# First loads and last transposes of an attention stage, put in another order

## The chip, the cores and the metric

The kernel runs on one core of one Trainium2 chip. The metric is the device time of one execution in microseconds (us); lower is better. A core has a matrix engine (TensorE, PE in the profile, with its weight loads as PEld), a vector engine (DVE), an activation engine (ACT), GpSimd (POOL) and a sync engine (SP), which here issues every transfer between DRAM and on-chip memory on one queue. Each engine runs its own instructions strictly in the order in which the program gives them, and waits where an operand is not there yet.

## The reference, cut to what matters

Attention inside chunks of 64 positions, then a soft mixture of experts on its result, then a gated feed-forward layer. All is float32; the last layer's weights are float64.

```python
def _attn_ref(q, k, v):                   # B, H, S, D = 8, 8, 576, 64
    scores = scale * np.matmul(q_c, k_c.transpose(0, 1, 2, 4, 3))   # chunks of 64
    scores = scores - np.max(scores, axis=-1, keepdims=True)
    attn = np.exp(scores)
    attn = attn / (np.sum(attn, axis=-1, keepdims=True) + 1e-09)
    out = np.matmul(attn, v_c)

def _moe_ref(x, phi, w1, w2):             # x is 4608 x 512, 8 experts of 4 slots
    logits = x @ phi
    d = np.exp(logits - logits.max(0, keepdims=True))
    d /= d.sum(0, keepdims=True) + 1e-09
    slot_input = d.T @ x
    # each expert e: slot_out[e] = np.maximum(slot_input[e] @ w1[e], 0) @ w2[e]
    # c = softmax of logits over the slots
    return c @ slot_out

def _moe2_ref(x, w_gate, w_val, w_out):   # 512 -> 1536 -> 512
    g = x @ w_gate
    return (g / (1.0 + np.exp(-g)) * (x @ w_val)) @ w_out
```

## The kernel before, in words

The order of every engine's instructions is the order in which the kernel is written (the scheduler is off). There are three stages.

**Stage one** is the attention with the token softmax of the mixture over all positions, run online. There are 36 tiles of 128 rows, taken in 18 passes (`p`) of two. Of tile `i` the queries and keys lie together in one of three buffers `qkbd` (`qk_bd[i % 3]`; part 0 holds the queries, parts 1 and 2 the keys of the upper and lower 64 partitions, each with zeros in the other half), its values in one of three buffers `vbd`. `load_qk` brings queries and keys into parts 0 and 1; `spread_k` then copies the lower half of part 1 into part 2 and clears what it copied from, and `spread_v` does the same with the values. Both run on POOL, but for the spread of tile 0's keys, which is DVE's.

A tile goes through `emit_scores` (8 products on PE into `s_ps`, then maximum and subtraction on DVE into `ssb`), `emit_pt` (4 transposes, exponential on ACT), `emit_pv` (products with the values into `xa_ps` and `xb_ps`; DVE scales them into `x_sb`, one for the two tiles of a pass), `emit_xt` (4 transposes into `xt_ps`; ACT copies them into `xt`). Four tiles make a group `g`, of which there are 9: `emit_logits` (16 products with `phi` into `lt_ps`, then running maximum and exponential), `emit_et` (one transpose, `e_ps`) and `emit_si` (4 products into `si_ps`, which DVE adds to `acc` with a factor). `load_qk(i + 3)` stands behind `emit_scores(i)` and waits for it, since it writes into the same buffer; `load_v(i + 3)` stands behind the products of tile `i` in the same way. So the sync engine's queue moves at the pace of PE, and PE waits for what the queue brings.

At the end of each pass `pump(1)` issues one load for the later stages: first `w_val`'s share (`load_gv0`; `w_gate`'s share is issued among the very first loads), then, from the third pass on, 1 MB of expert weights at a time (`w1t`, `w2t`), into 16 slots and, once stage one has released its buffers, 4 more.

The end of stage one is written out by hand: the last pass takes the first half of the last group's logits (tiles 32 and 33), adds up group 7, then transposes tiles 34 and 35, takes the second half of the logits, and goes through `emit_m1` (`mps`, the maximum over the four rows of a slot), `emit_et(8)`, `emit_m2` (`nps`, and the factor `al`, and from it `rsel`) and `emit_si(8)`. `warm(n)` puts in `n` products of the identity with itself, whose result nobody reads. The tag `t` has three PSUM buffers, which all the small results named here share.

**Stage two** is the experts: `sips` (L607) turns `acc` into the slots' inputs, then the products with `w1t` (`h_ps`, L636) and `w2t` (`so_ps`, L681). A weight slot is loaded anew when PE has read it. **Stage three** (from about 195 us on) is the gated layer, with float64 weights split into float32 pieces on the way; nothing in it is touched by the change.

Of the kernel before, what the change touches and what calls it, by code (L numbers as in the profile page):

```python
# [34 lines left out]
def tile_attn_softmoe_swiglu(  # L35
# [239 lines left out]
    with tc.manual_schedule():  # L275
# [22 lines left out]
        for u in range(3):  # L298
            load_qk(u)
            load_v(u)  # L300
            if u == 0:
                load_gv0(0, wp)
        nc.sync.dma_start(out=phi_sb, in_=phi.rearrange("(k p) s -> p k s", p=128))

        for i in range(NK):
            nc.vector.memset(qk_bd[i][top, 2], 0.0)
            nc.vector.memset(v_bd[i][top, 1], 0.0)
            if i == 0:
                make_identity(nc, ident)
# [161 lines left out]
        def emit_si(g):  # L471
            e = e_t.pop(g)
            ps = ps_t.tile([128, 512], F32, tag="t", name="si_ps")
            for jt in range(4):
                nc.tensor.matmul(
                    out=ps[32 * jt:32 * jt + 32, :],
                    lhsT=e[:, 32 * jt:32 * jt + 32],
                    rhs=x_t.pop(4 * g + jt),
                    start=True, stop=True,
                    tile_position=(0, 32 * jt),  # L480
                )
            if g:
# [24 lines left out]
        def emit_m2():  # L507
# [8 lines left out]
            nc.scalar.activation(out=al, in_=mrun[0], func=ACTF.Exp, bias=nm)  # L516
            rsel = sm.tile([128, 32], F32, tag="rsel", name="rsel", bufs=1)
            nc.vector.tensor_scalar(out=rsel, in0=sel_big[:, 0, :], scalar1=al, scalar2=None, op0=ALU.mult)
            tail['al'] = al
# [7 lines left out]
        spread_k(0, nc.vector)  # L527
        spread_k(1)
        spread_k(2)
        spread_v(0)  # L530
        spread_v(1)
        for i in range(2):
            emit_scores(i)
            load_qk(i + NK)
        spread_k(3)
        for i in range(2):
            emit_pt(i)
        NP = NTILE // 2
        for p in range(NP):
            if p < NP - 1:  # L540
                for i in (2 * p + 2, 2 * p + 3):
                    emit_scores(i)
                    if i + NK < NTILE:
                        load_qk(i + NK)
# [13 lines left out]
            if p >= 2 and p % 2 == 0:  # L558
                emit_logits(p // 2 - 1)
            if p >= 3 and p % 2:  # L560
                if p == NP - 1:
                    emit_logits(NG - 1, (0, 1), False)
# [10 lines left out]
        emit_xt(NTILE - 2)  # L573
        emit_xt(NTILE - 1)
        emit_logits(g, (2, 3))
        warm(4)
        emit_m1()
        nc.vector.tensor_copy(out=lt_all[:, g, :], in_=lt_t[g][:, 0:128])
        emit_et(g)
        warm(3)  # L580
        emit_m2()
        emit_si(g)
# [413 lines left out]
```

## Time and profile before

| what | us |
|---|---|
| median of 3 runs | 571.0 |
| lowest and highest | 570.22 and 571.45 |
| the profiled execution, its own time | 570.47 |
| its span, first to last instruction | 568.5 |
| PE busy | 540.1 (95% of the span) |
| PEld busy | 425.8 (75%) |
| DVE busy | 419.2 (74%) |
| POOL busy | 292.1 (51%) |
| ACT busy | 260.6 (46%) |
| share of the chain that ended last: PE, DMA, DVE | 80%, 12%, 4% |

The chain that ended last is followed back from the last instruction: at each step to what released it, or to the instruction before it on its engine. Busy shares are means over stages with different limits, and a PE that stands at a wait inside a row of products still counts as busy in part; what a change in one stage is worth is read from that stage's own rows. Times inside the trace count from the span's start. The granted clock of PE stands as a share of its upper level (2.4 GHz); half of it is the lower level (1.2 GHz).

### The profile page before, as it was taken

The page shows a single profiled execution, that of the slowest core. Times are in us where ns is not written, and L with a number is a line of the kernel's source. Part 1 is how long each engine was busy: PE and PEld are TensorE (multiplying, and loading weights), DVE is VectorE, ACT ScalarE, POOL GpSimd, SP SyncE. Part 2 cuts the span into 40 slices and gives each one's busy share as a digit, 9 for nine tenths or more (in the row PEclk, how much of TensorE's full clock was granted, in tenths as well). Part 3 has the DMA queues.
Part 4 walks back from the last instruction along what each step waited for, and adds up shares of the span by engine and source line. Part 5 has one row for each costly group of instructions (what it writes and reads, how often), then busy time and mean ns, then how long its engine had stood idle before and what let it go on. Part 6 is the DMA issues. An engine that isn't in the chain of part 4 may idle for free.

```text
span 568.5 us, 10116 instructions
## 1 busy us (share of the span) xinstructions
PE 540.1 (95%) x3823; PEld 425.8 (75%) x3823; DVE 419.2 (74%) x745; ACT 260.6 (46%) x500; POOL 292.1 (51%) x322
## 2 busy tenths in 40 slices
PE   3998999999999888999999999999999999999997
PEld 2877788777543556888888878887888788888885
DVE  5678887776475599989889878997998854433464
ACT  1233333334244576666665555554555543333331
POOL 3566766663100257656756556664676454343432
PEclk9999999999999998999999999999999999999999
DMA  7799999998899970202020240024000000122254
GB/s 256 261 305 345 359 376 369 359 375 310 323 381 379 390 269 1 74 1 74 0 75 0 76 149 1 0 75 148 1 1 1 0 2 0 44 105 75 74 186 184
DMA packets 37967, 91.03 MB, mean 160 GB/s; under 512 B 3104, under 2 KB 5152, under 8 KB 37920
## 3 DMA queue, kind: packets, MB, share of 16 engines
q1 hardware_dynamic: 37920, 90.40, 44.0%
q8 instruction: 30, 0.49, 0.3%
q14 instruction: 17, 0.14, 0.1%
HBM read 80.95 MB, written 9.44 MB: 159 GB/s over the span
## 4 chain that ended last, share of the span: by engine, by line
PE 80%; DMA 12%; DVE 4%; POOL 2%; issue 1%; ACT 1%; SPq 0%; POOLq 0%; DVEq 0%; ACTq 0%
PE o L877 17%; PE o L879 17%; PE o L878 17%; DMA qkbd<-in_qk_dram 5%; PE v_ps L833 4%; DMA vbd<-in_v_dram 4%; PE g_ps L833 4%; PE s_ps L337 4%; PE xa_ps L373 3%; PE h_ps L636 3%; DMA w2t<-in_moe_w_dram 2%; PE gg_ps L814 2%; PE pt_ps L359 2%; PE xt_ps L410 2%; PE so_ps L681 1%; PE lt_ps L428 1%
## 5 line engine op out<-in xcount | busy, mean ns | idle before, releaser
L846 POOL TENSOR_TENSOR lo_sb<-s_sb,hi_sb 128x512 fp32r<-128x512 f32 x106 | 140.6, 1326 | 134.1 <-ACT hi_sb L845 131.2
L877 PE MATMUL o<-whl,hi_sb 128*128 128x512 f32 x428 | 167.9, 392 | 2.5 <-DVE part L886 2.5
L879 PE MATMUL o<-whl,lo_sb 128*128 128x512 f32 x428 | 167.3, 391 | 0.5 <-POOL lo_sb L846 0.5
L878 PE MATMUL o<-whl,hi_sb 128*128 128x512 f32 x428 | 167.1, 391 | 0.0
L836 ACT ACTIVATE s_sb<-g_ps 128x512 f32<-128x512 f32 (+1 forms) x110 | 64.8, 591 | 153.6 <-PE g_ps L833 150.4
L837 DVE TENSOR_TENSOR s_sb<-s_sb,v_ps 128x512 f32<-128x512 f32 (+1 forms) x110 | 73.9, 673 | 78.1 <-ACT s_sb L836 76.6
L877 PEld LDWEIGHTS o<-whl,hi_sb 128*128 128x128 f32 x428 | 80.8, 189 | 22.4 <-DVE part L886 4.4
L879 PEld LDWEIGHTS o<-whl,lo_sb 128*128 128x128 f32 x428 | 80.6, 188 | 17.9 <-POOL lo_sb L846 0.9
L878 PEld LDWEIGHTS o<-whl,hi_sb 128*128 128x128 f32 x428 | 80.7, 189 | 16.3
L845 ACT ACTIVATE hi_sb<-s_sb 128x512 fp32r<-128x512 f32 (+1 forms) x110 | 67.6, 616 | 0.8 <-DVE s_sb L837 0.8
L890 DVE TENSOR_TENSOR part<-part,o 128x512 f32<-128x512 f32 x92 | 57.0, 676 | 2.6 <-PE o L879 2.6
L220 POOL TENSOR_TENSOR mt<-mt,ex 128x512 f32<-128x512 f32 x32 | 39.6, 1237 | 30.5 <-PE g_ps L833 14.4
L337 PE MATMUL s_ps<-qkbd 128*64 128x128 f32 x576 | 40.5, 293 | 12.3 <-POOL qkbd L322 6.5
L337 PEld LDWEIGHTS s_ps<-qkbd 128*64 128x64 f32 x576 | 33.9, 146 | 22.3 <-POOL qkbd L322 8.3
L207 DVE SCALAR_TENSOR_TENSOR ex<-raw,ex 128x512 uint16<-128x512 uint16 x32 | 47.7, 1490 | 0.1
L833 PE MATMUL v_ps<-c_t,g_st 128*128 128x512 f32 (+1 forms) x110 | 42.9, 393 | 3.1 <-ACT s_sb L836 2.5
L833 PE MATMUL g_ps<-c_t,g_st 128*128 128x512 f32 (+1 forms) x110 | 42.4, 388 | 0.1
L412 ACT ACTIVATE xt<-xt_ps 128x512 f32<-128x512 f32 (+1 forms) x36 | 19.4, 589 | 47.7 <-PE xt_ps L410 47.6
L321 POOL COPY qkbd<-qkbd 64x512 f32<-64x512 f32 x35 | 21.4, 612 | 30.5 <-DMA qkbd<-in_qk_dram 27.4
L202 DVE SCALAR_TENSOR_TENSOR mt<-mt,raw 128x512 f32<-128x512 f32 x32 | 34.6, 1081 | 0.0
L345 DVE TENSOR_REDUCE m<-s_ps 128x8 f32<-128x512 f32 x36 | 24.6, 684 | 12.1 <-PE s_ps L337 12.1
L194 DVE TENSOR_SCALAR mt<-raw 128x512 int32<-128x512 int32 x32 | 32.9, 1027 | 0.0
(144 smaller groups left out, 726.7 us busy)
## 6 DMA issues: line engine op xcount, KB each, us to landing
qkbd<-in_qk_dram SPq DMA_DIRECT2D x36, 512.0 KB, 5.7
w1t<-in_moe_w_dram SPq DMA_DIRECT2D x16, 1024.0 KB, 8.1
w2t<-in_moe_w_dram SPq DMA_DIRECT2D x15, 1024.0 KB, 10.7
vbd<-in_v_dram SPq DMA_DIRECT2D x36, 260.0 KB, 5.5
out_dram<-part SPq DMA_DIRECT2D x36, 256.0 KB, 2.2
raw<-in_moe_w_out_dram SPq DMA_DIRECT2D x6, 1024.0 KB, 7.7
raw<-in_moe_w_gate_dram SPq DMA_DIRECT2D x5, 1024.0 KB, 5.2
raw<-in_moe_w_val_dram SPq DMA_DIRECT2D x5, 1024.0 KB, 5.1
```

Source lines behind the costliest of these rows:

```text
L207: nc.vector.scalar_tensor_tensor(out=ex, in0=hh, scalar=0x8000, in1=ex, op0=ALU.bitwise_and, op1=ALU.bitwise_or)
L220: nc.gpsimd.tensor_tensor(out=m, in0=m, in1=p, op=ALU.mult)
L337: nc.tensor.matmul(out=sp[64 * cc:64 * cc + 64, j, :], lhsT=qk_bd[i % NK][:, 0, j, t0:t0 + 64], rhs=qk_bd[i % NK][:, 1:3, j, t0:t0 + 64], ...
L833: nc.tensor.matmul(out=ps[:, k], lhsT=g_st[:, c, gi, ff:ff + 128], rhs=c_blk(b)[:, k], start=True, stop=True)
L836: nc.scalar.activation(out=s[:, k], in_=gp[:, k], func=ACTF.Silu)
L837: nc.vector.tensor_tensor(out=s[:, k], in0=s[:, k], in1=vp[:, k], op=ALU.mult)
L845: nc.scalar.activation(out=hi[:, k], in_=s[:, k], func=ACTF.Copy)
L846: eng.tensor_tensor(out=lo[:, k], in0=s[:, k], in1=hi[:, k].bitcast(F32), op=ALU.subtract)
L877: nc.tensor.matmul(out=a, lhsT=hi[:, ts], rhs=w_hi, start=first, stop=False)
L878: nc.tensor.matmul(out=a, lhsT=hi[:, ts], rhs=w_lo, start=False, stop=False)
L879: nc.tensor.matmul(out=a, lhsT=lo[:, ts], rhs=w_hi, start=False, stop=last)
L890: nc.vector.tensor_tensor(out=p[:, t], in0=p[:, t], in1=a, op=ALU.add)
```

## The change

At the start, tile 0's load becomes three: the queries, the upper half of the keys into part 1, the lower half straight into part 2, each where the products read it, so that no spread of tile 0's keys is left. Tile 1's queries and keys follow at once, then the other first loads; the 512 KB of `w_gate`, which stood third, goes behind the load of tile 3. Ten products of the identity stand ahead of and between the first tiles' products, and tile 1's transposes go behind tile 2's scores. POOL spreads tile 0's values ahead of tile 2's keys.

At the end of stage one, the transposes of tiles 34 and 35 go into the last pass, ahead of the last group's logits, which are taken in one piece and ahead of group 7's `emit_si`. Seven products of the identity go away. `emit_m2` moves between the products and the additions of `emit_si(8)`, and `rsel` becomes a step of its own (`emit_m3`) behind them.

```diff
-        for u in range(3):
-            load_qk(u)
-            load_v(u)
-            if u == 0:
-                load_gv0(0, wp)
+        nc.sync.dma_start(out=qk_bd[0][:, 0], in_=qk[0, :, 0])
+        nc.sync.dma_start(out=qk_bd[0][top, 1], in_=qk[0, top, 1])
+        nc.sync.dma_start(out=qk_bd[0][bot, 2], in_=qk[0, bot, 1])
+        load_qk(1)
+        load_v(0)
+        load_qk(2)
+        load_v(1)
+        load_v(2)
...
+        make_identity(nc, ident)
+        nc.vector.memset(qk_bd[0][bot, 1], 0.0)
...
-            if i == 0:
-                make_identity(nc, ident)
...
-        def emit_si(g):
+        def emit_si(g, mid=None):
...
+            if mid:
+                mid()
...
-        spread_k(0, nc.vector)
+        warm(6)
         spread_k(1)
+        spread_v(0)
         spread_k(2)
-        spread_v(0)
         spread_v(1)
-        for i in range(2):
-            emit_scores(i)
-            load_qk(i + NK)
+        emit_scores(0)
+        load_qk(3)
+        load_gv0(0, wp)
+        warm(2)
+        emit_scores(1)
+        load_qk(4)
         spread_k(3)
-        for i in range(2):
-            emit_pt(i)
+        emit_pt(0)
+        warm(2)
...
                     emit_scores(i)
+                    if i == 2:
+                        emit_pt(1)
...
+            if p == NP - 1:
+                emit_xt(NTILE - 2)
+                emit_xt(NTILE - 1)
+                emit_logits(NG - 1)
             if p >= 3 and p % 2:
-                if p == NP - 1:
-                    emit_logits(NG - 1, (0, 1), False)
                 emit_si((p - 3) // 2)
...
-        emit_xt(NTILE - 2)
-        emit_xt(NTILE - 1)
-        emit_logits(g, (2, 3))
-        warm(4)
         emit_m1()
+        emit_et(g)
         nc.vector.tensor_copy(out=lt_all[:, g, :], in_=lt_t[g][:, 0:128])
-        emit_et(g)
-        warm(3)
-        emit_m2()
-        emit_si(g)
+        emit_si(g, emit_m2)
+        emit_m3()
         warm(3)
```

What this makes of PE's instructions at the start, before (`qkbd_98` to `_100` are the three buffers of tiles 0, 1, 2, then 3, 4, 5; the line is the kernel's):

```order
L337 MATMUL s_ps<-qkbd_98 64x128 x8
L337 MATMUL s_ps<-qkbd_99 64x128 x8
L359 MATMUL pt_ps<-ident,ssb 128x128 x8
L337 MATMUL s_ps<-qkbd_100 64x128 x8
L337 MATMUL s_ps<-qkbd_98 64x128 x8
L373 MATMUL xa_ps<-vbd_101,pt 64x130 x8
```

and PE's instructions at the same place now:

```order
L532 MATMUL warm<-ident 128x128 x6
L340 MATMUL s_ps<-qkbd_98 64x128 x8
L532 MATMUL warm<-ident 128x128 x2
L340 MATMUL s_ps<-qkbd_99 64x128 x8
L362 MATMUL pt_ps<-ident,ssb 128x128 x4
L532 MATMUL warm<-ident 128x128 x2
L340 MATMUL s_ps<-qkbd_100 64x128 x8
L362 MATMUL pt_ps<-ident,ssb 128x128 x4
L340 MATMUL s_ps<-qkbd_98 64x128 x8
L376 MATMUL xa_ps<-vbd_101,pt 64x130 x8
```

Ten identity products are new, and tile 1's transposes have moved behind tile 2's scores. The sync engine's queue at the start, before:

```order
L293 DMA qkbd_98<-in_qk_dram 128x1024
L296 DMA vbd_101<-in_v_dram 128x520
L117 DMA raw<-in_moe_w_gate_dram 128x4x256
L293 DMA qkbd_99<-in_qk_dram 128x1024
L296 DMA vbd_102<-in_v_dram 128x520
L293 DMA qkbd_100<-in_qk_dram 128x1024
L296 DMA vbd_103<-in_v_dram 128x520
L303 DMA phi_sb<-in_moe_phi_dram 128x4x32
L293 DMA qkbd_98<-in_qk_dram 128x1024
L293 DMA qkbd_99<-in_qk_dram 128x1024
```

and the sync engine's queue there now:

```order
L298 DMA qkbd_98<-in_qk_dram 128x512
L299 DMA qkbd_98<-in_qk_dram 64x512
L300 DMA qkbd_98<-in_qk_dram 64x512
L293 DMA qkbd_99<-in_qk_dram 128x1024
L296 DMA vbd_101<-in_v_dram 128x520
L293 DMA qkbd_100<-in_qk_dram 128x1024
L296 DMA vbd_102<-in_v_dram 128x520
L296 DMA vbd_103<-in_v_dram 128x520
L306 DMA phi_sb<-in_moe_phi_dram 128x4x32
L293 DMA qkbd_98<-in_qk_dram 128x1024
L117 DMA raw<-in_moe_w_gate_dram 128x4x256
L293 DMA qkbd_99<-in_qk_dram 128x1024
```

The gate weights (`raw`) have moved from third place to behind tile 3's load; from tile 4's load on, the queue has the same order as before. PE's instructions at the end of stage one, from the last pass's `e_ps` on, before:

```order
L462 MATMUL e_ps<-ident,et 128x128
L410 MATMUL xt_ps<-ident,x_sb 128x128 x8
L428 MATMUL lt_ps<-xt,phi_sb 32x128 x8
L475 MATMUL si_ps<-x_sb,e 32x512 x4
L410 MATMUL xt_ps<-ident,x_sb 128x128 x8
L428 MATMUL lt_ps<-xt,phi_sb 32x128 x8
L525 MATMUL warm<-ident 128x128 x4
L497 MATMUL mps<-ident,mx 1x128
L462 MATMUL e_ps<-ident,et 128x128
L525 MATMUL warm<-ident 128x128 x3
L509 MATMUL nps<-ident,nmrow 128x1
L475 MATMUL si_ps<-x_sb,e 32x512 x4
```

and PE's instructions there now:

```order
L465 MATMUL e_ps<-ident,et 128x128
L413 MATMUL xt_ps<-ident,x_sb 128x128 x16
L431 MATMUL lt_ps<-xt,phi_sb 32x128 x16
L478 MATMUL si_ps<-x_sb,e 32x512 x4
L502 MATMUL mps<-ident,mx 1x128
L465 MATMUL e_ps<-ident,et 128x128
L478 MATMUL si_ps<-x_sb,e 32x512 x4
L514 MATMUL nps<-ident,nmrow 128x1
L532 MATMUL warm<-ident 128x128 x3
```

The 16 transposes and the 16 logit products now stand in one piece each, and `nps` stands behind the last `si_ps`. On DVE, group 7's addition to `acc` now stands between the last maximum and the steps on `mps`.

## Rows read from the trace of the kernel before

**Rows 1.** Stretches: PE, PEld, DVE, ACT, POOL busy, granted clock, DMA share, GB/s

```profile
10.50:15.00 4.50, 4.03 (x24) 2.99 (x24) 1.38 (x2) 0.60 (x1) 3.67 (x7) 1.00 0.67 230
...
15.00:21.33 6.33, 6.33 (x73) 5.97 (x73) 3.96 (x8) 0.86 (x2) 3.84 (x8) 1.00 0.47 149
...
36.00:130.00 94.00, 89.94 (x1293) 73.67 (x1291) 75.52 (x178) 35.46 (x83) 60.21 (x105) 1.00 0.98 361
...
134.00:150.00 16.00, 15.29 (x171) 11.13 (x169) 8.78 (x30) 6.27 (x17) 2.67 (x7) 1.00 1.00 382
...
150.00:154.00 4.00, 3.66 (x34) 1.63 (x37) 1.29 (x10) 0.28 (x1) 0.32 (x2) 1.00 0.50 133
...
160.00:190.00 30.00, 29.18 (x246) 11.48 (x238) 19.61 (x72) 14.56 (x30) 3.09 (x6) 1.00 1.05 383
...
216.40:219.60 3.20, 3.20 (x9) 2.49 (x8) 2.06 (x5) 1.84 (x4) 2.31 (x2) 0.50 0.00 0
```

**Rows 2.** The sync engine's first four issues: start us, length us

```profile
0.74 0.38 SPq L293 DMA_DIRECT2D qkbd<-in_qk_dram  x1
1.18 0.42 SPq L296 DMA_DIRECT2D vbd<-in_v_dram  x1
1.64 0.43 SPq L117 DMA_DIRECT2D raw<-in_moe_w_gate_dram  x1
2.11 0.50 SPq L293 DMA_DIRECT2D qkbd<-in_qk_dram  x1
```

**Rows 3.** Those four loads in that order: KB, us from issue to landing

```profile
qkbd<-in_qk_dram SPq DMA_DIRECT2D x1, 512.0 KB, 3.4
...
vbd<-in_v_dram SPq DMA_DIRECT2D x1, 260.0 KB, 3.7
...
raw<-in_moe_w_gate_dram SPq DMA_DIRECT2D x1, 512.0 KB, 6.2
...
qkbd<-in_qk_dram SPq DMA_DIRECT2D x1, 512.0 KB, 7.0
```

**Rows 4.** Timeline of the start: start us, length us, engine, operation, idle before

```profile
1.01 0.29 POOL masks.py:199 TENSOR_SCALAR_AFFINE_SELECT ident<-ident 128x128 f32<-128x128 f32 x1
...
5.83 1.97 PE L337 MATMUL s_ps<-qkbd 128*64 128x128 f32 x16 [5.83 <-DVE qkbd L322]
...
9.25 0.61 POOL L321 COPY qkbd<-qkbd 64x512 f32<-64x512 f32 x1 [7.90 <-DMA qkbd<-in_qk_dram]
...
10.49 1.97 PE L337 MATMUL s_ps<-qkbd 128*64 128x128 f32 x16 [2.69 <-POOL qkbd L322]
...
15.02 3.58 PE L337 MATMUL s_ps<-qkbd 128*64 128x128 f32 x32
...
18.43 1.50 PE L373 MATMUL xa_ps<-vbd,pt 128*64 128x130 f32 x24
...
21.33 1.97 PE L337 MATMUL s_ps<-qkbd 128*64 128x128 f32 x32
```

**Rows 5.** Timeline of the end of stage one, columns as above

```profile
129.76 2.09 PE L337 MATMUL s_ps<-qkbd 128*64 128x128 f32 x32
...
139.22 1.08 ACT L412 ACTIVATE xt<-xt_ps 128x512 f32<-128x512 f32 x2 [0.16 <-PE xt_ps L410]
...
143.98 1.21 PE L428 MATMUL lt_ps<-xt,phi_sb 128*32 128x128 f32 x16
...
146.76 0.94 PE L525 MATMUL warm<-ident 128*128 128x128 f32 x6
...
147.94 1.06 PE L475 MATMUL si_ps<-x_sb,e 128*32 128x512 f32 x8
...
149.07 0.87 DVE L486 SCALAR_TENSOR_TENSOR acc<-acc,be,si_ps 128x256 f32<-128x256 f32 x2 [0.26 <-PE si_ps L475]
...
151.02 1.92 PE L636 MATMUL h_ps<-w1t,si_m 128*32 128x512 f32 x16 [0.34 <-DVE si_m L614]
```

**Rows 6.** Timeline of the end of stage two, columns as above

```profile
189.18 1.07 PE L681 MATMUL so_ps<-w2t,ht 128*32 128x512 f32 x8 [0.64 <-DMA w2t<-in_moe_w_dram]
```

More of the change, by code (lines that the diff above doesn't have):

```diff
@@ L516, in emit_m2, with emit_m3 @@
             nc.scalar.activation(out=al, in_=mrun[0], func=ACTF.Exp, bias=nm)
+            tail['al'] = al
+        def emit_m3():
             rsel = sm.tile([128, 32], F32, tag="rsel", name="rsel", bufs=1)
-            nc.vector.tensor_scalar(out=rsel, in0=sel_big[:, 0, :], scalar1=al, scalar2=None, op0=ALU.mult)
-            tail['al'] = al
+            nc.vector.tensor_scalar(out=rsel, in0=sel_big[:, 0, :], scalar1=tail['al'], scalar2=None, op0=ALU.mult)
             tail['rsel'] = rsel
```

## The prediction

> **What bounds the kernel now.** I read the busy time by stretch first, to see which resource is full where. In stage one proper (36 to 130 us) the transfers are busy 0.98 of the time, and PE 89.94 of 94 us [rows 1]: both are nearly full, so this stretch can hardly be made shorter, but it can start earlier. At its start it is neither: from 10.5 to 15 us the DMA share is 0.67, from 15 to 21.33 us 0.47 [rows 1], while PE is busy only because its rows last long. The timeline shows why [rows 4]: 32 records of scores take 3.58 us at 15.02 and 1.97 us at 21.33. The clock column reads 1.00 over the start, but by these lengths PE runs there at its lower level (1.2 GHz) and has reached the upper one (2.4 GHz) by about 18 us, after working almost without a break since 10.49. Since each load of queries and keys waits for the scores that free its buffer, the slow PE starves the queue. The first scores wait until 5.83 us for DVE's spread, the second until 10.49 for POOL's [rows 4].
>
> Behind stage one come weight loads at full rate (134 to 150 us, share 1.00), a hole (150 to 154 us, 0.50), and a full stretch (160 to 190 us, 1.05) [rows 1], at whose end PE waits for the last weights [rows 6]. The hole is there because all slots are full until PE begins with the expert products at 151.02 [rows 5] and frees the first. So the end of stage two hangs on two things: when stage one's loads are through, and when PE gets to 151.02. Stage three follows the same loads and then PE; it is shifted as a whole.
>
> **The start.** The first four loads are issued at 0.74, 1.18, 1.64 and 2.11 us [rows 2] and land 3.4, 3.7, 6.2 and 7.0 us later [rows 3], so at 4.14, 4.88, 7.84 and 9.11. One behind another, values cost 0.7 us, queries with keys 1.3, and the gate weights 3.0, more than twice as much for the same 512 KB. In the new order I add these up. Tile 0's three pieces move the bytes of the old load and need two issues more (0.4 us each, beside the transfer): landed by about 4.4. Then tile 1 at 5.7, values 0 at 6.4, tile 2 at 7.7, values 1 and 2 at 9.1, phi at 9.4 (estimate from its 64 KB at the rate of its neighbours), tile 3 at 10.7, the gate at 13.7, tile 4 at 15.0.
>
> PE: the identity is written by 1.30 us [rows 4], so the six products start there. Three such products are six records and take 0.94 us at the upper level [rows 5], so 0.3 each, and 0.6 at the lower one; six lie under the wait for tile 0 and end at about 4.8, some tenths after it. So scores 0 run from 4.8 to 6.8 (1.97 at the lower level). From landing to scores a spread costs 10.49 - 9.11 = 1.38 us, and POOL takes 1.2 us for each, copy and clear (0.61 and as much less as the clear is shorter) [rows 4]. POOL's chain: keys 1 to 7.0, values 0 to 8.2, keys 2 to 9.4, values 1 to 10.6, keys 3 to 11.9. PE: two products to 8.0, scores 1, transposes, two products, scores 2, transposes. If the clock has risen by about 9 us, as the 7.8 us from 10.49 to its old rise say, all this is ready by 11.9, and POOL decides: scores 3 end at 13.1, and the products with the values start there, against 18.43 before [rows 4]: 5.3 us earlier. The gate weights, moved to where queue and buffers were empty, then cost something: tile 4 lands at 15.0, its scores start at 16.4 against 21.33 (4.9 earlier), and tile 5's, behind two more spreads on POOL, at 18.6 against 22.4 (half way through that row), 3.8 earlier. From the queue's side the bound is the idle transfer time to be won back: 0.33 x 4.5 + 0.53 x 6.33 = 4.8 us [rows 1]. I take **4.4 us**, the middle of 3.8 and 4.9. The lead is kept, since from tile 4's load on every queue has its old order and 36 to 130 us is bound by transfers whose number is the same.
>
> The lower bound: PE stays at 1.2 GHz up to the values. Before, it went at that level from scores 1 at 10.49 to the values at 18.43 in 7.9 us [rows 4]. From scores 1 at 8.0 the same work and two more products (1.2) end at 17.1: 1.3 us earlier than 18.43. I keep 1.3 to 4.9.
>
> Here a page speaks against the split of tile 0. The trace: values 0, 260 KB, landed 0.74 us behind the load ahead of them [rows 2, 3], about 360 GB/s, so a small load queued behind others pays no start of its own. The Trainium skill, "DMA: Bandwidth & Descriptors", section "Bandwidth", wants at least 1 MiB in one transfer and gives a 64 KB one 138 GB/s. By that rate the 512 KB in pieces would take 3.8 us in place of 1.3; the trace does not agree, but it becomes a rival below.
>
> **The end of stage one.** Before, the second half of the logits starts at 143.98 and lasts 1.21 [rows 5]. Now tiles 34 and 35 are transposed right behind 32 and 33, whose copies take ACT from 139.22 to 140.30 [rows 5]. Two more copies on ACT (one of them half as wide, the other half on DVE) end at about 141.3, 16 logit products run beside them from 141.0 to 142.5. That is 2.7 us earlier than 145.2. Some is given back. Group 7's four products (1.06, as in [rows 5]) now stand behind the logits, to 143.5; its addition on DVE (0.87 as two halves [rows 5], I take 0.8) ends at 144.4 and holds up both the steps on `mps` and the buffer of `e_ps`. Then `e_ps` and ACT's copy to 145.1, group 8's products to 146.2, `nps`, `nm`, `al` to 147.0, the additions beside them to 147.6, `rsel` to 147.8, `sips` and its copy to 149.2. So the expert products start at 149.2 in place of 151.02: **1.8 us**. Of the products removed, the three of 146.76 [rows 5] lay on the old path, and nothing has to take their place. The bounds: 0, if the additions end last and buffers wait for each other at two more places (0.9 each, as the DVE row); and 2.0, the idle time in the hole, 0.50 x 4 [rows 1], since more than that the loads behind it cannot take up.
>
> **Sum.** 4.4 + 1.8 = 6.2 us. The profiled execution took 570.47 us (span 568.5, 1.97 around it) and would take 564.3; the median, 0.53 higher, goes from 571.0 to **564.8**. One term of chance: in stage three PE drops to half its clock from 216.4 to 219.6 us [rows 1] after a wait; where the new times fall otherwise, that costs up to 1.6 us more or that much less.
>
> **The rivals.**
> 1. The clock rises late. PE stays at 1.2 GHz until the first values. The lead is 1.3, the end gives 1.8: 571.0 - 3.1 = 567.9. For it: the old rise took 7.8 us of work. Against it: six products from 1.3 us on give it that by 9 us.
> 2. The pieces of tile 0 land 2.5 us late (3.8 less 1.3). Scores 0 begin at 7.2, and the lead falls to some 1.9: 567.3. This is what the rate on the skill's page would bring.
> 3. The lead is given back, because in the full stretch transfers and PE wait for each other anyway: only the end counts, 569.2.
> 4. The change does not do what it says: lead given back, and the end's gain hidden in the hole, since the loads of 134 to 150 us are not through earlier: 571.0.
> 5. Slower. The place is the loop of stage one. Its 16 passes from 15.02 [rows 4] to 129.76 us [rows 5] take 7.2 us each. With the gate's slow transfer now between tiles 3 and 4, the loop could settle into an order in which each pass finds its keys later. One that takes 7.7 us, 0.5 more, loses 8.5 in 16 passes: 571.0 - 6.2 + 8.5 = 573.3. It decides from 0.46 us a pass (6.2 plus 1.1, through 16). Against it: the queue's order from tile 4 on is the old one.
>
> **How the numbers follow.** Chances: the forecast 0.60, rivals 1 to 5 0.14, 0.05, 0.08, 0.08 and 0.05. A difference of 0.2% (1.1 us) is about what a measurement of this kernel can tell from no change. Faster by more than that are the forecast and rivals 1 to 3: 0.87; the same, rival 4: 0.08; slower, rival 5: 0.05. The range starts at 562.5 (4.9 and 2.0 us gained, 1.6 less lost in stage three) and reaches to 569.0: it holds the forecast, rivals 1 and 2 and some of 3.
>
> **What would show it.** Scores 0 before 5 us; the first values at about 13; scores of tile 4 at 16 to 17; a DMA share above 0.9 from 6 to 21 us; the loop's passes 7.2 us long; the first expert products at about 145 us (151.02 less 6.2); the last wait for weights 6 us earlier. It is wrong if the first values start after 16 us (rival 1 or 2), if they start early and the expert products still come later than 148 us (rival 3 or 5), or if those come at 145 and the last weights no earlier than before (rival 4).

## The result, and the profile after

The changed kernel takes 564.2 us (median of 4 runs, 563.28 to 565.04) beside 570.6 us for the kernel before. The ratio is 0.991, 95% interval 0.988 to 0.994, so by the ratio the gain is 5.3 us, between 3.7 and 6.7. The same kernel, run again on another occasion with six runs, gave 0.994 (0.991 to 0.996), a gain of 3.7 us, between 2.5 and 5.0. By the medians alone the two differences are 6.4 and 3.8 us. Faster, then, as forecast, by some 4 to 5 us.

The page of the profiled execution: its span, PE's busy time, and then the span in 40 slices, with the granted clock and the busy share of the transfers in tenths (9 is 90% or more) and the GB/s that they moved.

```profile
span 562.2 us, 10134 instructions
...
PE 537.7 (96%) x3829; PEld 424.6 (76%) x3829; DVE 418.8 (74%) x744; ACT 260.5 (46%) x500; POOL 291.6 (52%) x322
...
PEclk9999999999999989999999999999999999999999
DMA  8899999998999930202010240114000000122254
GB/s 282 295 342 382 361 374 368 382 343 319 367 386 378 394 142 1 75 2 75 3 73 1 76 150 1 31 45 150 0 2 0 2 0 1 70 79 76 85 187 178
```

The first slices carry more: 282, 295, 342, 382 GB/s, where the kernel before had 256, 261, 305, 345 on its page. PE is as full as it was.

The timeline of the start, PE and POOL (start us, length us, engine, operation, idle time before and what ended it), answers [rows 4]:

```profile
1.36 2.93 PE L532 MATMUL warm<-ident 128*128 128x128 f32 x12 [1.36 <-POOL cbias L321]
4.93 1.09 PE L340 MATMUL s_ps<-qkbd 128*64 128x128 f32 x16 [0.65 <-DVE sel_big L313]
...
8.50 1.09 PE L340 MATMUL s_ps<-qkbd 128*64 128x128 f32 x16 [1.83 <-POOL qkbd L325]
...
10.97 1.09 PE L340 MATMUL s_ps<-qkbd 128*64 128x128 f32 x16 [0.34 <-POOL qkbd L325]
...
14.19 1.09 PE L340 MATMUL s_ps<-qkbd 128*64 128x128 f32 x16 [1.54 <-POOL qkbd L325]
15.11 1.50 PE L376 MATMUL xa_ps<-vbd,pt 128*64 128x130 f32 x24
...
18.01 2.23 PE L340 MATMUL s_ps<-qkbd 128*64 128x128 f32 x32
```
```profile
7.26 0.61 POOL L324 COPY qkbd<-qkbd 64x512 f32<-64x512 f32 x1 [5.92 <-DMA qkbd<-in_qk_dram]
...
12.95 0.61 POOL L324 COPY qkbd<-qkbd 64x512 f32<-64x512 f32 x1 [0.89 <-DMA raw<-in_moe_w_gate_dram]
```

Scores 0 start at 4.93 and last 1.09: the clock is at its upper level already. POOL gets tile 1's keys at 7.26 and tile 3's only at 12.95, after 0.89 us of waiting for a transfer. That row names the gate weights (`raw`), but these landed only at 14.2; what landed just ahead of it, at 12.8, was tile 3's load. The first values start at 15.11, which is 3.3 us ahead of 18.43, not 5.3. The busy time by stretch answers [rows 1]; the last three columns are the granted clock, the DMA share and GB/s:

```profile
5.80:10.50 4.70, 2.87 (x33) 2.29 (x28) 2.21 (x4) 0.28 (x1) 2.93 (x6) 1.00 0.94 326
10.50:15.00 4.50, 2.62 (x36) 2.09 (x36) 1.94 (x3) 0.91 (x2) 2.63 (x5) 1.00 1.04 386
15.00:21.00 6.00, 5.95 (x94) 5.25 (x90) 5.14 (x11) 1.08 (x2) 3.77 (x7) 1.00 0.79 257
21.00:28.00 7.00, 6.35 (x88) 5.41 (x86) 4.93 (x12) 2.07 (x4) 5.39 (x11) 1.00 0.83 314
```

The idle stretch of 10.5 to 15 us is full (1.04 for 0.67), that behind it mostly (0.79 for 0.47), and 21 to 28 us stands at 0.83, where the kernel before had 0.99.

The end of stage one and the last wait for weights, PE, which answer [rows 5, 6]:

```profile
131.71 1.55 PE L376 MATMUL xa_ps<-vbd,pt 128*64 128x130 f32 x24
...
139.39 0.30 PE L465 MATMUL e_ps<-ident,et 128*128 128x128 f32 x1 [0.60 <-DVE acc L491]
140.05 1.06 PE L478 MATMUL si_ps<-x_sb,e 128*32 128x512 f32 x8 [0.37 <-ACT e L467]
...
142.61 1.08 PE L616 MATMUL sips<-rsel,acc 128*128 128x32 f32 x8 [0.32 <-DVE rsel L526]
144.03 1.92 PE L645 MATMUL h_ps<-w1t,si_m 128*32 128x512 f32 x16 [0.34 <-DVE si_m L623]
...
182.24 1.07 PE L690 MATMUL so_ps<-w2t,ht 128*32 128x512 f32 x8 [0.80 <-DMA w2t<-in_moe_w_dram]
```

The last pass of the kernel before began its values here:

```profile
136.50 1.55 PE L373 MATMUL xa_ps<-vbd,pt 128*64 128x130 f32 x24
```

Now it begins them at 131.71, and the experts start at 144.03, 12.32 us later (14.52 before). The experts are 7.0 us earlier than 151.02, the last wait for weights 6.9 earlier than 189.18, the end of the span 6.3.

### The profile page after: what moved, and what is told of

It is laid out like the page before. It is cut to its first block, busy times and chain, and to the rows that moved or that the text cites. A ratio compares the mean times of both kernels' runs of the same rounds, so it can differ in the third digit from the quotient of the medians.

```text
span 562.2 us, 10134 instructions
## 1 busy us (share of the span) xinstructions
PE 537.7 (96%) x3829; PEld 424.6 (76%) x3829; DVE 418.8 (74%) x744; ACT 260.5 (46%) x500; POOL 291.6 (52%) x322
## 4 chain that ended last, share of the span: by engine, by line
PE 80%; DMA 10%; DVE 5%; POOL 2%; ACT 1%; issue 1%; SPq 0%; POOLq 0%; DVEq 0%; ACTq 0%
PE o L886 17%; PE o L887 17%; PE o L888 17%; PE v_ps L842 4%; PE g_ps L842 4%; DMA qkbd<-in_qk_dram 4%; PE s_ps L340 3%; DMA vbd<-in_v_dram 3%; PE xa_ps L376 3%; PE h_ps L645 3%; DMA w2t<-in_moe_w_dram 2%; PE gg_ps L823 2%; PE xt_ps L413 2%; PE pt_ps L362 2%; PE so_ps L690 1%; PE lt_ps L431 1%
## 5 line engine op out<-in xcount | busy, mean ns | idle before, releaser
L340 PEld LDWEIGHTS s_ps<-qkbd 128*64 128x64 f32 x576 | 30.9, 137 | 15.9 <-POOL qkbd L325 7.3
L340 PE MATMUL s_ps<-qkbd 128*64 128x128 f32 x576 | 37.2, 277 | 5.9 <-POOL qkbd L325 5.2
L324 POOL COPY vbd<-vbd 64x520 f32<-64x520 f32 x36 | 22.4, 623 | 18.0 <-DMA vbd<-in_v_dram 12.3
```

What stands on the lines that cost most here:

```text
L324: eng.tensor_copy(out=t[bot, o], in_=t[bot, i])
L340: nc.tensor.matmul(out=sp[64 * cc:64 * cc + 64, j, :], lhsT=qk_bd[i % NK][:, 0, j, t0:t0 + 64], rhs=qk_bd[i % NK][:, 1:3, j, t0:t0 + 64], ...
```

## The experiments

For twelve further runs the table gives, from each profile, where the first values start, where the last pass starts its values, how long after that the first weight slot comes free (the sync engine's issue of the first `w2t` after it), and where PE's clock falls to its lower level. The ratio is to the kernel before, run on the same chip (medians of 570.1, 569.9 and 570.2 us for the runs named e1, e2 and e3). Each fall takes 1.7 us of PE's work (the sum of what the granted clock lacks over it).

| run | time us | ratio, 95% interval | first values | last pass | to first slot | falls at us |
|---|---|---|---|---|---|---|
| before | 570.6 | | 18.43 | 136.50 | 15.65 | 216 |
| after | 564.2 | 0.991 (0.988, 0.994) | 15.11 | 131.71 | 13.45 | 196, 210 |
| e1_start | 567.9 | 0.995 (0.992, 0.998) | 15.63 | 134.54 | 15.65 | 201, 215 |
| e1_tail | 567.6 | 0.994 (0.991, 0.996) | 17.91 | 134.76 | 14.19 | 147 |
| e1_whole | 565.0 | 0.988 (0.984, 0.992) | 14.65 | 131.95 | 14.05 | 145 |
| e1_noprod | 565.0 | 0.989 (0.985, 0.993) | 16.07 | 133.28 | 13.86 | 146, 211 |
| e2_gate3 | 566.2 | 0.993 (0.991, 0.995) | 16.50 | 133.76 | 14.10 | 146, 211 |
| e2_order | 565.6 | 0.993 (0.991, 0.995) | 14.37 | 133.88 | 13.44 | 199, 212 |
| e2_tailprod | 565.2 | 0.992 (0.990, 0.995) | 14.62 | 131.61 | 13.75 | none |
| e2_zero | 565.3 | 0.992 (0.990, 0.994) | 15.43 | 131.78 | 14.22 | 144 |
| e3_after | 566.4 | 0.994 (0.991, 0.996) | 14.83 | 134.13 | 14.20 | 147 |
| e3_prod | 565.1 | 0.992 (0.989, 0.994) | 15.07 | 133.74 | 13.75 | 211 |
| e3_fill | 565.8 | 0.994 (0.991, 0.996) | 14.85 | 131.63 | 13.45 | 196, 210 |
| e3_both | 564.4 | 0.991 (0.988, 0.993) | 15.11 | 134.47 | 13.74 | 211 |

### The two parts alone

`e1_start` has the new start and the old end of stage one, `e1_tail` the old start and the new end.

> The new start with the old end of stage one. If the two terms are independent, as the sum took them, the last pass starts its values 4.8 us earlier than before (131.7 us), the expert products come 4.8 us earlier than 151.02, so at 146.2, and the time is 570.6 - 4.8 = 565.8 us, give or take 1.6 for the clock in stage three. Rival (lead given back in the full stretch of weight loads): the expert products come at 146.2, but the last wait for weights is less than 3 us earlier, and the time is above 567.5.

> The old start with the new end of stage one. If the terms are independent: first values of the last pass at 136.5 us as before, expert products 2.2 us earlier (148.8), the last wait for weights about 2 us earlier (the hole in the transfers before was 2.2 us), time 570.6 - 2.0 = 568.6 us. Rival (the loads of 134 to 150 us are not through when the first slots come free, so the gain is hidden): time 570.6.

Measured: 567.9 and 567.6 us, by the ratios gains of 2.9 (1.4 to 4.4) and 3.5 us (2.1 to 5.0). Added up they are 6.4, and the two together gave 5.3 and 3.7, so within the intervals the parts add, and each is worth something by itself. `e1_tail` came out 1 us faster than its 568.6. `e1_start` missed its 565.8: its last wait for weights is only 1.7 us earlier than before, as the rival said, but not for the rival's reason. From the last pass to that wait it takes 52.9 us, before 52.7; nothing was given back there. The last pass itself is only 2.0 us earlier. And `e1_tail`, whose loop is that of before, has its last pass 1.7 us earlier than before. So the loop's length differs between profiles of the same code, and a lead read from one pair of profiles, such as the 4.8 us above, is not the start's worth.

### How far the loop scatters

> The changed kernel once more, unaltered, to see how far its own profiles differ. Three other profiles with the same start have the last pass begin its values at 131.6, 131.8 and 134.5 us, against 131.71. If the lead is settled by the start, it is 131.7 again, within 0.3; if the loop's transfers scatter, it lies anywhere from 131.6 to 134.5. Time 564.2 to 565.

The last pass starts at 134.13, 2.4 us later than in the first profile of this kernel, although its first values came 0.3 us earlier. Six profiles have this start unaltered (after, e3_after, e1_start, e2_tailprod, e2_zero, e3_prod): their last passes lie between 131.61 and 134.54, with a mean of 132.9, against 135.6 for the two with the old start. The chip alone does not settle it: the four profiles named e3, all of one chip, lie between 131.63 and 134.47. The two profiles of the changed kernel start the values of the fifth pass at the same time (40.68 and 40.64 us). Then the transfers run at different rates, as busy time by stretch shows, first of after, then of e3_after (columns as above):

```profile
50.00:60.00 10.00, 10.00 (x147) 8.37 (x145) 8.41 (x20) 4.32 (x9) 7.73 (x14) 1.00 0.96 357
60.00:70.00 10.00, 9.66 (x145) 7.80 (x137) 8.93 (x20) 4.37 (x11) 6.38 (x12) 1.00 1.00 377
70.00:80.00 10.00, 9.98 (x153) 8.81 (x150) 8.71 (x21) 3.96 (x11) 7.67 (x13) 1.00 1.00 368
```
```profile
50.00:60.00 10.00, 10.00 (x147) 8.17 (x143) 8.37 (x20) 4.41 (x9) 7.37 (x12) 1.00 0.95 337
60.00:70.00 10.00, 8.11 (x109) 6.25 (x105) 8.20 (x19) 4.16 (x10) 5.69 (x10) 1.00 0.98 347
70.00:80.00 10.00, 9.70 (x156) 8.40 (x158) 8.05 (x19) 2.71 (x7) 6.47 (x12) 1.00 0.96 337
```

The share is 0.95 to 1.00 in both, but 337 to 347 GB/s stand beside 357 to 377. Why the same loads on the same queue run 6 to 8% slower in one execution stays open. What it means is plain: the start's lead is 2.7 us as a mean over profiles, an uncertain figure, since the two with the old start differ by 1.7 themselves, and 3.1 us where the first values start (15.1 beside 18.2).

### What the first values wait for

`e2_gate3` puts the gate weights in third place again, the rest as changed:

```diff
         load_v(0)
+        load_gv0(0, wp)
         load_qk(2)
...
         load_qk(3)
-        load_gv0(0, wp)
```

> The changed kernel with the gate weights in third place again (behind the values of tile 0, ahead of tile 2). Theory P (the 3.0 us that this load took before are those of its place in time, some slow microseconds of the queue between 4 and 8 us, and not its own): behind tile 1 and values 0 it lands in 1.4 to 1.6 us, tiles 2 and 3 land about that much later than in the changed kernel, tile 3 at 14.2, the first values at some 16.5 in place of 15.1, and the time is 565.6, 1.4 above the changed kernel. Theory G (as the prediction had it, the gate load itself is slow): it takes 3 us there, tile 3 lands at 15.8, first values at 18, time 567.

The loads of this run from 2.39 us on, in the order of the queue: tile 1, values 0, gate, tile 3 (KB, us from issue to landing), and its first values:

```profile
qkbd<-in_qk_dram SPq DMA_DIRECT2D x1, 512.0 KB, 4.2
```
```profile
vbd<-in_v_dram SPq DMA_DIRECT2D x1, 260.0 KB, 4.3
```
```profile
raw<-in_moe_w_gate_dram SPq DMA_DIRECT2D x1, 512.0 KB, 6.3
```
```profile
qkbd<-in_qk_dram SPq DMA_DIRECT2D x1, 512.0 KB, 6.8
```
```profile
15.57 1.09 PE L341 MATMUL s_ps<-qkbd 128*64 128x128 f32 x16 [1.49 <-POOL qkbd L326]
16.50 1.50 PE L377 MATMUL xa_ps<-vbd,pt 128*64 128x130 f32 x24
```

Issued at 2.39, 3.02, 3.49 and 7.35 us, they land at 6.6, 7.3, 9.8 and 14.15. In the changed kernel tile 1, tile 3 and the gate behind it land like this:

```profile
qkbd<-in_qk_dram SPq DMA_DIRECT2D x1, 512.0 KB, 4.7
```
```profile
qkbd<-in_qk_dram SPq DMA_DIRECT2D x1, 512.0 KB, 6.7
```
```profile
raw<-in_moe_w_gate_dram SPq DMA_DIRECT2D x1, 512.0 KB, 7.6
```

Issued at 2.40, 6.06 and 6.64, they land at 7.1, 12.8 and 14.2. The gate takes 1.5 us there, 2.5 in third place, and took 3.0 in third place before [rows 2, 3]. But it is not always the gate that is slow. In the changed kernel it is tile 1, which takes 2.3 us behind tile 0 (4.8 to 7.1). In `e2_gate3` tile 1 and values 0 take 1.3 and 0.7 us, and the gate behind them, from 7.3 to 9.8, is the slow one. In `e1_whole`, told below, where the gate stands behind tile 3, the values of tile 0 take 2.5 us for their 260 KB (issued at 1.64, landed at 7.8, tile 1 ahead of them at 5.3):

```profile
vbd<-in_v_dram SPq DMA_DIRECT2D x1, 260.0 KB, 6.2
```

So in each of these profiles some load that goes through between 4 and 10 us takes 1 us or more longer than such a load takes later, whichever load it is, and most of the gate's 3.0 us belonged to the place and not to the load. Why transfers are slow there stays open. Theory P had tile 3 and the first values right to a tenth, since 512 KB more ahead of tile 3 delay it by 1.4 us; its 1.4 to 1.6 us for the gate itself was wrong, and so were theory G's 15.8 and 18. The time, 566.2, lies between the two.

The landing of tile 3 sets the first values: it stands 2.35 us ahead of them in both, and 2.3 to 2.4 us in five more profiles of this order (2.7 in e1_start, whose clock rose late, and 3.2 in e1_noprod, whose clock had not risen at all by then).

`e1_whole` loads tile 0 in one piece and lets DVE spread its keys, `e2_order` in addition puts values 2 and phi behind tile 3 and the gate behind tile 5:

```diff
-        nc.sync.dma_start(out=qk_bd[0][:, 0], in_=qk[0, :, 0])
-        nc.sync.dma_start(out=qk_bd[0][top, 1], in_=qk[0, top, 1])
-        nc.sync.dma_start(out=qk_bd[0][bot, 2], in_=qk[0, bot, 1])
+        load_qk(0)
...
         warm(6)
+        spread_k(0, nc.vector)
```

and, in `e2_order` alone:

```diff
         load_v(1)
-        load_v(2)
-        nc.sync.dma_start(out=phi_sb, in_=phi.rearrange("(k p) s -> p k s", p=128))
...
         load_qk(3)
-        load_gv0(0, wp)
+        load_v(2)
+        nc.sync.dma_start(out=phi_sb, in_=phi.rearrange("(k p) s -> p k s", p=128))
...
                         load_qk(i + NK)
+                    if i == 2:
+                        load_gv0(0, wp)
```

> The changed kernel with tile 0's queries and keys in one load again and DVE's spread of its keys; all else as changed. If the pieces are what made tile 1 land at 7.1 us in place of 5.7 (2.3 us behind tile 0, where the trace of before has 1.3 for such a load), tile 0 lands near 4.1, tile 1 near 5.6, tile 3 near 11.4, the first values start about 1 us earlier than 15.11, and scores 0 only near 5.7. Theory A (the lead of the loop is the transfer time won back in the first 42 us): the last pass gains up to 1 us more, time 563.2 to 564.2. Theory B (the lead is that of the first values): the same 1 us. Rival (the pieces cost nothing, the transfers are slow there anyway): tile 1 lands at 7 us as before, and scores 0 come 0.8 us later, time 564.2 to 565.

> Tile 0 in one load (as in the run before, whose time was that of the changed kernel), values 2 and phi behind tile 3's load, the gate weights behind tile 5's. Nothing is left out. If the landing of tile 3 sets the first values, it lands some 0.9 us earlier than 12.4 (324 KB fewer ahead of it), the first values start at 13.7 in place of 14.65, the last pass keeps that lead, and the time falls by 0.9 us against the run with tile 0 in one load, to some 564. Rival (what is taken out early has to come later, the loop is bound by the bytes that its first 42 us move): no change of the last pass, 564.9.

In one piece tile 0 lands at 4.04 us (the last of the three pieces at 4.77 in after, at 4.7 to 5.5 over the profiles), tile 1 at 5.3, near the 5.6 of theories A and B, but tile 3 at 12.36 and not 11.4, since the slow transfer is now the values'. The gate lands at 13.74, and scores 0 start 0.9 us later. Eight profiles have the pieces and this order, with tile 3 at 12.2 to 13.1 and the first values of seven of them at 14.62 to 15.63 (16.07 in e1_noprod); with the one load tile 3 lands at 12.36 and 12.8 and the first values start at 14.65 and, in e3_both, at 15.11. So the split neither costs nor buys anything that shows: it gains up to 1 us for scores 0, on which the first values do not wait. With values 2, phi and the gate put back as well, tile 3 lands at 11.15, but scores 0 ran at the lower clock (1.98 us from 5.83 on) and kept its load from being issued before 7.85; the transfers stand at 0.72 from 5.8 to 10.5 us, and the first values start at 14.37, not 13.7. Its last pass lies within the loop's scatter, so whether the lead lasts is not settled by it.

`e1_noprod` leaves out the ten identity products of the start.

> The changed kernel without the ten identity products of the start (their result is read by nobody). If they are what raises TensorE's clock early, scores 0 take 1.97 us in place of 1.09, and the rows of scores stay near that length until some 7 us of work have passed, to about 15 us; the first values come some 2 us later than 15.11 and the lead of the last pass shrinks from 4.8 to about 3: time 566. Rival (transfers set the pace, TensorE waits for tiles 1 to 3 at either clock): the lead stays within 0.5 us of 4.8, time 564.2 to 564.7.

The scores of the first four tiles last 1.97 or 1.98 us each. Tile 3 lands at 12.9, within the range of the others; its scores take 0.9 us longer than at the upper clock, and the first values start at 16.07, 1 us later than the mean of the six, not 2. The last pass (133.28) lies within the loop's scatter, and the time does not differ. With the products the clock is up at scores 0 in 4 of the 11 profiles that have them (after among them); in the others scores 0 last 1.97 or 1.98 and the rise comes by 8.3 to some 13 us. Neither shows in the first values (14.65 to 15.43 and 14.37 to 15.63, e2_gate3 apart), which wait for tile 3 either way, but in e2_order, where PE itself is late.

### The expert products

`e2_tailprod` and `e3_prod` are one kernel: five identity products more, in places where PE waits (`idle` writes into columns that nobody reads).

```diff
             nc.tensor.transpose(mps[0:1, 0:128], mrun[0], ident)
+            idle(mps, 2)
...
         emit_et(g)
+        idle(tail['mps'], 1)
...
-        warm(3)
+        warm(4)
...
+        idle(sips, 1)
         sipv = sips[:, 0:128].rearrange("p (k s) -> p k s", k=4)
```

> The changed kernel with five identity products more at the end of stage one, in places where TensorE waits (two behind mps, one behind e_ps, one more of the last three, one behind sips). In three of four profiles with the new end the clock fell at the expert products, for 3.4 us, and never in two with the old end, which had seven such products. Theory W (the removed products kept the clock up there): no fall between 140 and 152 us, the first slot comes free 13.5 us after the last pass begins its values, or up to 0.3 later for the products themselves, and over the runs the time is some 0.5 to 1 us below the changed kernel: 563.5. Rival (the fall is chance, or it is hidden by the loads): the fall is there again or the time stays 564.2 to 564.8.

> The changed kernel with the five identity products more at the end of stage one, again, with more rounds and beside the changed kernel on one chip. Theory W (they keep the clock up at the expert products, where it fell in five of seven profiles of the new end without them): no fall between 140 and 152 us, and the time lies 0.5 to 1.5 us below the changed kernel's of the same chip. Rival (what the fall takes is hidden by the weight loads): no difference in time, within 0.5 us.

The first expert products and the busy time around them, first of e1_tail, then of e3_prod:

```profile
147.07 3.54 PE L637 MATMUL h_ps<-w1t,si_m 128*32 128x512 f32 x16 [0.34 <-DVE si_m L615]
```
```profile
142.00:144.00 2.00, 1.20 (x9) 0.29 (x9) 1.14 (x7) 0.28 (x1) 0.38 (x2) 1.00 1.02 412
144.00:146.00 2.00, 1.68 (x15) 1.39 (x12) 1.09 (x4) 0.29 (x1) 0.00 (x0) 1.00 1.03 410
...
147.00:150.60 3.60, 3.53 (x17) 0.65 (x17) 0.33 (x5) 0.28 (x1) 0.00 (x0) 0.53 0.77 290
```
```profile
146.36 1.92 PE L653 MATMUL h_ps<-w1t,si_m 128*32 128x512 f32 x16 [0.34 <-DVE si_m L631]
```
```profile
141.00:143.00 2.00, 1.84 (x14) 0.66 (x12) 1.22 (x7) 0.28 (x1) 0.37 (x2) 1.00 1.03 416
143.00:145.00 2.00, 1.91 (x18) 1.62 (x14) 1.09 (x4) 0.30 (x1) 0.00 (x0) 1.00 1.03 412
...
146.00:149.60 3.60, 3.26 (x31) 1.08 (x34) 1.46 (x10) 0.28 (x1) 0.11 (x1) 1.00 0.81 296
```

In e1_tail PE is busy 1.20 and 1.68 of 2 us in the two stretches, then works at 0.53 of its clock and takes 3.54 us for 16 records; in e3_prod it is busy 1.84 and 1.91, keeps its clock, and they take 1.92. Of the nine profiles with the new end as it is, six show this fall, of the three with five products more none, of the two with the old end none. In the six the first slot comes free 13.9 to 14.2 us after the last pass began, in the other three 13.4. The product behind `sips` costs 0.3 (13.75), as the copies behind it now wait for it too. Three profiles are few: with a fall in two of three, three without one would come by chance once in 27 times. In time, e2_tailprod's 565.2 is not the 563.5 of theory W, and its ratio of 0.992 lies between the changed kernel's two (0.991 and 0.994); e3_prod lies 1.3 us below e3_after by the medians of the same chip, as theory W has it, but the intervals overlap. The fall is shown, its price in the whole time is not settled.

### Stage three

`e2_zero` adds products with zeros into open sums where PE waits at 195 and 207 us:

```diff
+        def zeros(t, x, n):
+            for _ in range(n):
+                nc.tensor.matmul(out=acc_t[t][0:104, :], lhsT=zpad, rhs=x, start=False, stop=False)
...
+                        if i == 0 and t == 2:
+                            zeros(t, x, 4)
...
+                if t == 2:
+                    zeros(t, hi, nz)
...
-                emit_out(*seq[n - LAG])
+                emit_out(*seq[n - LAG], nz=8 if n - LAG == 2 else 0)
```

> The changed kernel with products of zeros, added to sums that are open, in two waits of stage three (four where TensorE waits for g_st at 195 us, eight where it waits for part at 207 us); the result stays what it was. If a fall of the clock after such a wait costs what it takes away (3.4 us at half speed, 1.7 us each), neither fall appears, the granted clock stays at 1.00 from 180 to 230 us, and the time is 1.7 to 3.4 us below the changed kernel: 561 to 562.5. Rival (VectorE sets the pace there, TensorE catches up in its next waits): no fall, and the time stays within 0.7 us of 564.2.

PE's rows around the second wait:

```profile
207.56 2.02 PE L864 MATMUL o<-hi_sb,pad_l 128*104 128x512 f32 x8
210.28 0.50 PE L893 MATMUL o<-whl,hi_sb 128*128 128x512 f32 x1 [0.71 <-DVE part L904]
210.62 0.39 PE L894 MATMUL o<-whl,hi_sb 128*128 128x512 f32 x1
```

The eight products fill all but 0.71 us of the wait for DVE, the clock stays at 1.00 from 180 to 230 us, and the time is 565.3. The theory's 561 to 562.5 missed; the rival has the mechanism, though 565.3 lies a little above its 564.9. That the clock held is not shown to be the zeros' doing, since e1_tail, e1_whole, e2_tailprod and e3_after have no fall in stage three either, and no zeros. What the falls cost is read from all the profiles: from the start of the last row of eight products into `so_ps` to the start of the last row of `part` on DVE it takes 373.5 to 373.6 us in the five with no fall in stage three, 373.6 to 373.7 in the five with a fall only at 211 to 216, and 374.1 to 374.2 in the four with falls at 196 to 201 and again later. So the later fall alone costs nothing that shows, which fits the waits for DVE behind it, and the two together cost 0.5 us. No profile has the earlier one alone.

The two places hang together. The three profiles of the new end that keep the clock at the experts without the five products (after, e2_order, e3_fill) are the ones that lose it at 196 to 199; the six that lose it at the experts keep it there.

### Filling the queue, and all together

```diff
-            pump(1)
+            pump(2 if p == 0 else 1)
```

> The changed kernel with the 1 MB weight loads of the loop issued from the second pass on in place of the third; the loop's last one moves up, so the bytes stay the same. Between 21 and 28 us the changed kernel's transfers are busy 0.83 of the time, 1.2 us idle. Theory A (the loop is bound by the bytes that must come, so idle transfer time at its start is its lead): the share there rises above 0.95, the last pass starts its values 1 us or more earlier relative to what it has loaded, and the time falls by about 1 us, to 563.2. Rival (the tile loads that queue up behind the 1 MB come 2.8 us later, and the passes wait for them): the second pass starts its scores later, and the time is 564.2 to 566.

> The three edits that looked worth something, together: tile 0 in one load, the five identity products at the end of stage one, and the weight loads from the second pass on. If each gives what its theory says (0.4, 1 and 1 us), the time is 2 us or more below the changed kernel, at 562. If only the products do, 563.4; if none does, 564.2.

In e3_fill the share from 21 to 28 us is 1.01 (0.83), and by 120 us 0.9 MB more is through than in the changed kernel, with the last pass at the same time (131.63). It comes back at the end of stage one, in the busy time by stretch:

```profile
142.00:143.00 1.00, 0.68 (x7) 0.49 (x6) 0.47 (x2) 0.00 (x0) 0.00 (x0) 1.00 1.04 414
143.00:144.00 1.00, 0.66 (x10) 0.55 (x13) 0.28 (x4) 0.00 (x0) 0.20 (x1) 1.00 0.48 180
144.00:145.00 1.00, 1.00 (x12) 0.37 (x16) 0.20 (x3) 0.28 (x1) 0.00 (x0) 1.00 0.13 41
145.00:146.00 1.00, 1.00 (x13) 0.20 (x3) 0.00 (x0) 0.00 (x0) 0.03 (x1) 1.00 0.02 8
146.00:147.00 1.00, 1.00 (x11) 0.45 (x14) 0.88 (x5) 0.00 (x0) 0.08 (x1) 1.00 0.52 68
```

From 143.5 us the loads are through and the queue stands until PE frees the first slot at 145.08. The changed kernel has 1.05 and 1.00 in the second and third of these stretches. The idle time was moved from the start into the hole, and the time is 565.8, no better. The next passes' scores start no later for the moved loads (24.60 and 31.53 us, 24.75 and 31.73 in the changed kernel), so the rival's reason does not hold either, though its time does. With all three edits the time is 564.4, a ratio of 0.991, and 2.0 us below e3_after by medians on the same chip (six runs each, 563.72 to 566.51 and 564.87 to 567.75). That is the 564.2 expected if none of the three gives anything, not 562. It may be a little faster than the changed kernel, but the intervals overlap, so this is not shown.

## Why the prediction held, and where its steps did not

The time (564.2 for 564.8) and the direction held. Of the signs that the forecast named, scores 0 (4.93), the experts (144.03 for about 145) and the last weights (6.9 earlier for 6) came as said; the first values (15.1 for 13), scores 4 (18.0 for 16 to 17) and the DMA share from 15 to 21 us (0.79 for 0.9) did not. Step by step:

**The start, 4.4 us, was too large.** It measures 2.7 to 3.1 in the profiles and 2.9 in the time of e1_start. The step that failed is the adding up of landings: the 3.0 us of the gate load were taken for its own price and moved behind tile 3 with it. They were mostly the price of its place, and fell in the changed kernel on tile 1 (landed at 7.1, forecast 5.7) and so on every load up to tile 3 (12.8, forecast 10.7). A plain count of bytes would have told: phi, with the same 2892 KB ahead of it and in it, landed at 12.2 before (issued at 4.28, 7.9 us to landing). With that, POOL no longer decides; it waits 0.89 us for tile 3's keys, and the first values start at 15.1, not 13.1. The bound from idle transfer time (4.8) was an upper bound; that the last pass of the first profile met it was luck, since the six profiles of this start scatter by 2.9 us around a smaller lead.

**The clock at the start** did rise early, earlier than forecast in this profile, later in others; where it rose only at some 13 us (e1_start) the first values stood 2.7 us behind tile 3's landing in place of 2.35, so that cost about 0.3. Rival 1's condition was made in e1_noprod: the lead of the first values fell to 2.1 us (16.07 beside the mean of 18.2), not 1.3.

**The pieces** landed at 4.8 in after and at 4.7 to 5.5 over the profiles, not at 4.4, and tile 3 lands no later with them than the profiles scatter (12.2 to 13.1, and 12.36 with the one load), so rival 2 falls. Its page, the Trainium skill's "DMA: Bandwidth & Descriptors", section "Bandwidth", wants large transfers, and its rate had made the pieces 2.5 us dearer; the landings do not bear that out for loads that queue up one behind another. The price was also set too high there: the rate that it used is the page's for 64 KB, and the pieces have 256 and 128 KB.

**The end of stage one, 1.8 us,** was right in size, and hides two things. PE gains 2.2 us from the last pass to the experts in every profile with the new end (12.3 us for 14.5), or 1.9 with the five products more (12.6). And the sentence that nothing has to take the place of the products removed was wrong: in six of nine profiles the clock falls at the experts, and the first slot comes 0.4 to 0.8 us later for it. From the last pass to that last row of `part` the new end takes 424.6 to 424.8 us without that fall and 424.9 to 425.7 with it, the old one 426.2 and 427.0: a gain of 1.9 or 1.2 by the means. With the five products it takes 424.3 to 424.5. By its time, 3.5 us (2.1 to 5.0), e1_tail gained more than these rows explain; where the rest comes from stays open.

**Stage three's 1.6 us either way** was the price of a fall without its cover. A fall at 211 to 216 us alone costs nothing that shows, one at 196 to 201 with one behind it half a microsecond. The Trainium skill, "TensorE: Matmul & The Clock Gate", section "HAM oscillation — how this bites in real kernels", counts half of such a stretch as wall time; where PE waits for DVE behind it, the measured 0 and 0.5 us decide.

**Rivals 3 to 5.** The full stretch gave back nothing: from the last pass to the last weights the two profiles with the old end take 52.7 and 52.9 us. The end's gain is not hidden, as e1_tail shows. The passes did not get longer: from the first to the last values it is 116.6 and 119.3 us in two profiles of the changed kernel, 118.1 before.

So the terms as the profiles have them, 2.7 and 1.2 to 1.9, make 3.9 to 4.6 us, beside 5.3 and 3.7 measured. The forecast of 6.2 was about 2 us too high. That 564.2 lies so near 564.8 is luck: the first runs lay on the kind side, in the profile of after the loop was short and the clock held at the experts, and six later runs of the same kernel have a median of 566.4.

## What to carry to other kernels

When a load seems dear in a trace, see whether another load in the same place and time is dear too, before its price is moved with it; the count of bytes ahead of a landing is the safer sum. Two profiles of one kernel may differ in a transfer-bound loop by more than half of what the change is worth (2.4 us here), so take a lead from several, and from the row that the change reaches first. Work that only keeps an engine's clock up is to be judged by what follows it: the same fall cost 0.4 to 0.8 us where slots wait for PE, and at most half a microsecond, for two of them, in stage three, where PE waits for DVE.

## What the runs showed of the hardware

The granted clock at the first expert products fell in six of nine executions of the same piece of code and held in three, in e1_tail with no wait of PE over 0.6 us in the 13 us ahead of it, and e2_order, with the same waits, kept its clock; so such a fall is not settled by the program alone. The rise at the start, too, came with scores 0 in 4 of 11 profiles and by some 13 us in the rest. Between 4 and 10 us after the start a load took 1 us or more longer than such a load does later, and it was tile 1, values 0 or the gate weights, by the run (2.3, 2.5 and 2.5 us). And transfers at a share of 0.95 to 1.00 moved 337 to 377 GB/s in the same loop.
